# Agent attention with a gated convolution on one core: fold order, agent-value tiles and the agents' table changed

## The chip, the cores and the metric

The kernel runs on 1 core of one Trainium2 chip. The time is device microseconds of one execution; 431.86 us is the median of 3 runs before the change (431.13 to 434.68). The engines are TensorE (PE, with its weight loads listed apart as PEld), VectorE (DVE), ScalarE (ACT), GpSimd (POOL) and SyncE (SP), which issues most of the DMAs.

## The reference

Two stages. In the attention, 49 agents look at 12,800 keys and gather values; then 12,800 queries look at the 49 agents and take their gathered values. The result goes through a causal depthwise convolution of 5 taps, a sigmoid gate and two 128 x 128 matrices. Batch 4, 128 channels, all float32 in and out.

```python
def sm(a, b):
    s = scale * (a @ b.transpose(0, 2, 1))
    s = s - s.max(-1, keepdims=True)
    e = np.exp(s)
    return e / (e.sum(-1, keepdims=True) + 1e-09)
a2k = sm(agents, k)
agent_v = a2k @ v
q2a = sm(q, agents)
x = q2a @ agent_v
...
for k in range(K):
    gate_pre += conv_w[k][None, None, :] * xp[:, k:k + S, :]
gate = 1.0 / (1.0 + np.exp(-gate_pre))
val = x @ w_val
return (gate * val @ w_out).astype(np.float32)
```

## The kernel before

The sequence of each batch is cut into 10 units of 1280 positions (`UNIT`) and 25 chunks of 512 (`CH`). The attention output x is never formed in 128 channels. It is q2a @ agent_v, so agent_v (49 rows) is folded into the weights that follow: the fold builds, per batch, matrices of 49 agents by 128 channels for each convolution tap and for the value matrix, and the chunks multiply the 49 normalised query weights by them. Each is split into two float16 parts, stacked in the rows of one matmul.

For the program a unit or chunk of work has a letter, and the list `work` holds them in the order of PE:

- `("k", b, u)`, `key_scores`: 8 matmuls with 32-column weights (half the 64 padded agents, four groups of 320 keys in four column tiles of the PE array side by side) into one of two PSUM banks `sc`, which alternate from one score unit to the next. ACT copies the bank to `ks`, DVE takes the maximum (`kmx`).
- `("v", b, u)`, `agent_values`: ACT's exponentials `e`, DVE's 32 x 32 block transposes `eT`, then 10 matmuls of 128 rows by 64 columns (one per block of 128 keys) by 129 value columns, the last of them ones for the denominator. They accumulate in `av`; even blocks go to PSUM rows 0 to 63, odd ones to 64 to 127.
- `("q", b, u)`, `queries`: scores as for the keys, then on DVE sT (transposes, which free the `sc` bank), qmx, on POOL the subtraction, on ACT the exponential, on DVE qsm, qr and the product qw, and the two float16 parts pt by ACT and POOL.
- `("t", b, u)`, `transposes`: pt into x1. The first four units (`PE_FIRST`) by 10 PE transposes into an `sc` bank, which ACT and DVE copy out; the others by a DMA transpose. Five DMAs (`shifts`) then copy 20 rows of x1, each shifted by a tap, to x2.
- `("fold", b)`, one of five steps of `fold_weights`: (1) `av` is copied (L491), halves are added by two matmuls, DVE normalises to `avT`, POOL makes `gw`, DVE the gate's scale. (2) PE multiplies by the value matrix, and DVE and ACT write the split weights `wst`. (3) PE transposes `wst` 8 times, DVE and ACT copy to `stat`; POOL scales the output matrix to `wo`. (4) PE transposes `wo` (L629); DVE finds its scale and splits it into `wsp` (L634 to L643). (5) PE transposes `wsp` twice (L655), DVE copies to `wo16`.
- `("g", t)`, `("a", t)`, `("o", t - 2)`: gate and value matmuls of a chunk (they need `stat`; the value matmuls write the bank `val`, read by DVE's `h`, L868), and the projection two chunks later, which needs `wo16`. The small PSUM results of batch 0's fold use the banks `out`, `val` and `gate` in turn.

`Plan` sets the order of the other engines: it simulates a list schedule with the given durations, with PE kept in the order of `work` and each change of a step's `key` on PE charged 0.12 us, and issues the steps by their start in that plan. The loads (k, q, v units) follow the order of `work` through 11 slots (`NLOAD`), issued from SP up to 11 units ahead; 8 DMAs may be out at a time in the plan.

For batch 0, all 10 key units run first, then two query units, then 10 value units. The fold of batch 0 is followed directly by chunk 0. `KEYS_FIRST` says how many of batch 1's key units stand ahead of the others around that fold. The keys of the next batch are spread over the early chunks of this one, its values over the later ones, two value units behind a score unit at five places (`at[AV0 + u // 2]`).

Of the kernel before, what the change touches and what calls it, by code (L numbers as in the profile page):

```python
# [19 lines left out]
BLK = 32  # L20
# [21 lines left out]
EARLY = ((1, 4), (2, 5), (4, 6))  # L42
SINGLE = 4
KEYS_EARLY = 2
KEYS_FIRST = 2
AV0 = 4
PE_FIRST = 4
PE_TURNS = ()
# [123 lines left out]
def tile_agent_attention_gated_conv(  # L172
# [81 lines left out]
    fold = const.tile([P, AP_], F32, name="fold")  # L254
    ag_sb = const.tile([P, B, AP_], F32, name="ag_sb")
    tiny = const.tile([P, NBLK], F32, name="tiny")
    nc.sync.dma_start(out=ag_sb, in_=agT.rearrange("b c a -> c b a"))
    make_identity(nc, ident)
    make_identity(nc, ident16)
    nc.vector.tensor_tensor(  # L260
# [88 lines left out]
    def load(kind, b, u):  # L349
        i = taken[0] % NLOAD  # L350
        taken[0] += 1
        slot_of[kind, b, u] = i
        if kind == "v":
            dst, src = ld[i], vP[b, u].rearrange("p n c -> p (n c)")
        else:
            dst = ld[i][:, 0:UNIT]
            src = (kT if kind == "k" else qT)[b, :, u * UNIT : (u + 1) * UNIT]
        add("dma", 0.4, lambda: nc.sync.dma_start(out=dst, in_=src), (), [("ld", i)], 1.57)

    def score_matmuls(b, src, out):  # L360
        for j in range(2):
# [10 lines left out]
    def transpose_blocks(out, in_):  # L372
        nc.vector.transpose(  # L373
            out=out.rearrange("p n (j i) -> p j n i", j=2),
            in_=in_.rearrange("p j (n i) -> p j n i", i=BLK),
        )


    def key_scores(b, u):
        i = slot_of["k", b, u]  # L380
        ps, at = bank()
        km = ("kmx", b % 2)
        add("pe", 1.07, lambda: score_matmuls(b, ld[i], ps), [("ld", i)], [at], key="sc")

        first = b == 0 and u == NU - 1

        def copy():
            add(
                "act", 0.64, lambda: nc.scalar.copy(out=ks[:, u], in_=ps[:, :, 0:GT]),  # L389
                [at] + ([(*km, u)] if first else []), [("ks", u)],  # L390
            )

        if not first:
            copy()
        src = ps[:, :, 0:GT] if first else ks[:, u]
# [52 lines left out]
    def agent_values(b, u):  # L448
# [8 lines left out]
                    bias=kbias[b % 2][:, j : j + 1], scale=SCALE,  # L457
                )

        def matmuls():  # L460
            for n in range(NBLK):
                o = (n % 2) * AP_
                nc.tensor.matmul(  # L463
                    out=av[o : o + AP_, 0 : C + 1], lhsT=et[:, n, :], rhs=vt[:, n, :],
                    start=(u == 0 and n < 2), stop=(u == NU - 1 and n >= NBLK - 2),
                )

        add("act", 1.0, exps, [("ks", u), ("kbias", b % 2)], [("e", u % 2)])
        add("dve", 0.84, lambda: transpose_blocks(et, e), [("e", u % 2)], [("eT", u % 3)])
        add(  # L470
            "pe", 1.07, matmuls, [("eT", u % 3), ("ld", i)], ["av"], key="av"
        )


    av2 = const.tile([P, C + 1], F32, name="av2")
# [191 lines left out]
    def queries(b, u):  # L667
# [7 lines left out]
        add("pe", 1.07, lambda: score_matmuls(b, ld[i], ps), [("ld", i)], [at], key="sc")  # L675
# [270 lines left out]
    for u in range(NU):  # L946
        work.append(("v", 0, u))
        if u == T_AT:
            work.append(("t", 0, 0))
    work += [("fold", 0), ("k", 1, 0), ("fold", 0), ("k", 1, 1), ("fold", 0)]  # L950
    after = {
        0: [("fold", 0), ("q", 0, 2), ("fold", 0), ("t", 0, 1), ("q", 0, 3)],
        1: [("t", 0, 2)],
        2: [("t", 0, 3)],
    }
# [6 lines left out]
    for b in range(B):  # L962
# [6 lines left out]
        if b + 1 < B:  # L969
            u0 = KEYS_FIRST if b == 0 else KEYS_EARLY  # L970
            part = (NU - u0 + 3) // 4
            for n, u in enumerate(range(u0, NU)):
                before[t0 + at[n // part]].append(("k", b + 1, u))
            for t in MAX_AT:
                behind[t0 + t].append(("max", b + 1))
            for u in range(NU):
# [81 lines left out]
```

## Time and profile before

| what | us |
|---|---|
| median of 3 runs | 431.86 |
| runs | 431.13 to 434.68 |
| profiled execution, whole | 431.22 |
| its span, first to last instruction | 429.4 |
| PE busy in the span | 402.9 |
| DVE / ACT / POOL busy | 297.0 / 300.4 / 224.3 |

The span is what the profile's times count from; the profiled execution's own time is 1.8 us longer. A row of the timeline or of the chain gives the start, the length, engine, what is written and read with its line, and a count where equal instructions were merged; in brackets stands the idle time before it and what ended it. Matmuls overlap, so lengths of merged rows run past the start of the next row. A float32 matmul is recorded twice, with two weight loads.

### The profile page before, as it was taken

How to read it: one execution, taken by the hardware profiler on the slowest of the kernel's cores; microseconds unless marked ns; L12 is line 12 of the kernel's file. 1: busy time of each engine (PE TensorE's matmuls, PEld its weight loads, DVE VectorE, ACT ScalarE, POOL GpSimd, SP SyncE). 2: the span in 40 equal slices, each digit the busy share in tenths (PEclk: the TensorE clock that was granted, in tenths of full speed). 3: DMA queues.
4: the chain of work that ended last, by engine and by line, in shares of the span. 5: the costliest groups of instructions: out<-in, count | busy, mean ns of one | idle time of the engine just before them, and what ended most of it. 6: DMA issues, size and time to landing. Idle time of an engine off the chain costs nothing.

```text
span 429.4 us, 8968 instructions
## 1 busy us (share of the span) xinstructions
PE 402.9 (94%) x3307; PEld 194.8 (45%) x3307; DVE 297.0 (69%) x555; ACT 300.4 (70%) x520; POOL 224.3 (52%) x239
## 2 busy tenths in 40 slices
PE   3978888999999999999999999999999999999995
PEld 1357333345565444444555544445555544434443
DVE  3776879886786877578666887678666787566231
ACT  1464536678976577778876676778876577777875
POOL 1002246564466665544557665553356466687553
PEclk9999989999999999999999999999999999999999
DMA  8999999999999999999999999999999999887743
GB/s 288 422 415 415 371 350 337 297 285 309 343 358 294 249 270 289 307 309 305 340 329 356 292 323 292 320 312 334 306 330 257 289 291 287 215 199 173 192 156 122
DMA packets 76158, 128.07 MB, mean 298 GB/s; under 512 B 51644, under 2 KB 51900, under 8 KB 76116
## 3 DMA queue, kind: packets, MB, share of 16 engines
q1 hardware_dynamic: 76056, 127.41, 96.0%
q8 instruction: 26, 0.43, 0.4%
q14 instruction: 16, 0.13, 0.1%
q10 hardware_dynamic: 60, 0.10, 0.1%
HBM read 79.25 MB, written 26.21 MB: 246 GB/s over the span
## 4 chain that ended last, share of the span: by engine, by line
PE 65%; DMA 13%; DVE 12%; ACT 5%; issue 3%; SPq 1%; POOL 1%; DVEq 0%; ACTq 0%; POOLq 0%
PE gate L828 20%; PE sc L363 13%; PE av L463 6%; PE gate L832 4%; PE val L855 4%; PE val L859 4%; PE out L898 4%; PE out L899 4%; PE out L900 4%; DMA ld<-qT 3%; DMA ld<-vP 3%; DVE h L868 2%; ACT e L455 2%; DMA ld<-kT 2%; DMA outT<-ob 2%
## 5 line engine op out<-in xcount | busy, mean ns | idle before, releaser
L879 POOL TENSOR_TENSOR hl<-h,hh 128x512 f16<-128x512 f32 (+1 forms) x101 | 117.0, 1160 | 121.3 <-ACT hh L874 113.7
L828 PE MATMUL gate<-x,stat 128*128 128x512 f16 (+1 forms) x500 | 124.4, 378 | 2.4 <-ACT th L841 2.3
L868 DVE SCALAR_TENSOR_TENSOR h<-th,val 128x512 f32<-128x512 f32 x100 | 67.7, 677 | 69.1 <-PE out L899 46.1
L363 PE MATMUL sc<-ld,ag_sb 128*32 128x320 f32 x1280 | 102.0, 452 | 10.0 <-DMA ld<-kT 8.0
L912 ACT ACTIVATE ob<-out,oscale 128x512 f32<-128x512 f32 x98 | 67.2, 686 | 23.5 <-PE out L900 17.4
L841 ACT ACTIVATE th<-gate,unscale 128x512 f32<-128x512 f32 x100 | 68.3, 683 | 19.7 <-PE gate L832 18.0
L828 PEld LDWEIGHTS <-stat 128*128 128x128 f16 x505 | 45.6, 97 | 66.4 <-issue 19.0
L874 ACT CAST hh<-h 128x512 f16<-128x512 f32 (+1 forms) x101 | 61.4, 608 | 13.1 <-DVE h L868 12.4
L684 POOL TENSOR_TENSOR qw<-sT,qmx 128x490 f32<-128x490 f32 x40 | 41.5, 1038 | 50.2 <-DVE qmx L679 50.1
L363 PEld LDWEIGHTS sc<-ld,ag_sb 128*32 128x32 f32 x1280 | 37.0, 112 | 62.8 <-issue 22.5
L463 PE MATMUL av<-ld,eT 128*64 128x129 f32 x800 | 49.5, 275 | 1.7 <-DMA ld<-vP 1.4
L389 ACT COPY ks<-sc 128x640 f32<-128x640 f32 x40 | 27.7, 691 | 32.7 <-PE sc L363 30.6
L463 PEld LDWEIGHTS av<-ld,eT 128*64 128x64 f32 x800 | 43.7, 136 | 11.7 <-issue 7.3
L726 POOL TENSOR_TENSOR pt<-qw,pt 128x490 f16<-128x490 f32 x40 | 44.7, 1119 | 3.8 <-ACT pt L713 3.1
L455 ACT ACTIVATE e<-ks,kbias 128x320 f32<-128x320 f32 x80 | 39.0, 553 | 6.1 <-DVE kbias L444 3.3
L373 DVE STREAM_TRANSPOSE eT<-e 128x640 f32<-128x640 f32 x40 | 33.6, 842 | 11.4 <-ACT e L455 5.9
L373 DVE STREAM_TRANSPOSE sT<-sc 128x640 f32<-128x640 f32 x40 | 33.3, 834 | 10.8 <-PE sc L363 10.6
L398 DVE TENSOR_REDUCE kmx<-ks 128x2 f32<-128x640 f32 x39 | 31.4, 817 | 11.8 <-ACT ks L389 11.8
L832 PE MATMUL gate<-x,stat 100*128 100x512 f16 x100 | 38.0, 380 | 0.8 <-DMA x<-x 0.8
L855 PE MATMUL val<-x,stat 128*128 128x512 f16 x100 | 37.8, 378 | 0.1
L859 PE MATMUL val<-x,stat 100*128 100x512 f16 x100 | 37.8, 378 | 0.0
L898 PE MATMUL out<-hh,wo 128*128 128x512 f16 x98 | 37.1, 379 | 0.0
(125 smaller groups left out, 392.1 us busy)
## 6 DMA issues: line engine op xcount, KB each, us to landing
ld<-vP SPq DMA_DIRECT2D x40, 645.0 KB
ld<-kT SPq DMA_DIRECT2D x40, 640.0 KB
ld<-qT SPq DMA_DIRECT2D x40, 640.0 KB
outT<-ob SPq DMA_DIRECT2D x48, 512.0 KB
x<-x SPq DMA_DIRECT2D x90, 100.0 KB
x<-x SPq DMA_DIRECT2D x18, 50.0 KB
outT<-ob SPq DMA_DIRECT2D x3, 256.0 KB
x<-pt SPq DMA_TRANSPOSE x36
```

Of the source, the lines that this page charges most:

```text
L363: nc.tensor.matmul(out=out[g * BLK : (g + 1) * BLK, j, 0:GT], lhsT=ag_sb[:, b, j * BLK : (j + 1) * BLK], rhs=src[:, g * GT : (g + 1) * GT] ...
L373: nc.vector.transpose(out=out.rearrange("p n (j i) -> p j n i", j=2), in_=in_.rearrange("p j (n i) -> p j n i", i=BLK),)
L463: nc.tensor.matmul(out=av[o : o + AP_, 0 : C + 1], lhsT=et[:, n, :], rhs=vt[:, n, :], start=(u == 0 and n < 2), stop=(u == NU - 1 and n >= ...
L828: nc.tensor.matmul(out=pg, lhsT=stat[:, k, :], rhs=x1[:, c : c + w], start=(k == 0), stop=False,)
L832: nc.tensor.matmul(out=pg, lhsT=stat[0 : TAPS * X2R, TAPS + 1, :], rhs=x2[0 : TAPS * X2R, o2 : o2 + w], start=False, stop=True,)
L841: lambda: nc.scalar.activation(out=th, in_=pg, func=AF.Tanh, scale=unscale[:, 0:1]),
L855: nc.tensor.matmul(out=pv, lhsT=stat[:, TAPS, :], rhs=x1[:, PAD + n0 : PAD + n0 + w], start=True, stop=False,)
L859: nc.tensor.matmul(out=pv, lhsT=stat[0 : TAPS * X2R, TAPS + 2, :], rhs=x2[0 : TAPS * X2R, o2 : o2 + w], start=False, stop=True,)
L868: lambda: nc.vector.scalar_tensor_tensor(out=h, in0=th, scalar=1.0, in1=pv, op0=ALU.add, op1=ALU.mult),
L874: "act", 0.16 + 0.42 * scale, lambda: nc.scalar.copy(out=hh, in_=h),
L879: lambda: nc.gpsimd.tensor_tensor(out=hl, in0=h, in1=hh, op=ALU.subtract),
L912: lambda: nc.scalar.activation(out=ob[:, o : o + w], in_=po, func=AF.Copy, scale=oscale),
```

## The change

Six things:

1. The agents' table is stored as c x b x a, and its load is issued by ACT, not SP.
2. The load of the last value unit of batch 0 is split into two halves (a second key `ld2`), and its 10 blocks into two steps on PE, each waiting for its half.
3. The agent-value matmuls use two 32-column tiles in place of one of 64, so 20 in place of 10 per unit, with tile positions like the scores'. Their `key` in the plan becomes that of the scores, "sc".
4. Around batch 0's fold: `("q", 0, 2)` moves from behind chunk 0 to behind the second fold step; the key unit `("k", 1, 2)` stands behind the third in place of ahead of chunk 0, and `("k", 1, 3)` behind chunk 0.
5. The fourth fold step (the transpose of `wo`) moves ahead of chunk 0's gate.
6. The other key units of batch 1 start one place later (`at[n // part + (b == 0)]`).

```diff
-KEYS_FIRST = 2
+KEYS_FIRST = 4
...
-    nc.sync.dma_start(out=ag_sb, in_=agT.rearrange("b c a -> c b a"))
+    nc.scalar.dma_start(out=ag_sb, in_=agT)
...
-        add("dma", 0.4, lambda: nc.sync.dma_start(out=dst, in_=src), (), [("ld", i)], 1.57)
+        parts = [(dst, src, [("ld", i), ("ld2", i)])]
+        if (kind, b, u) == ("v", 0, NU - 1):
+            h = VW // 2
+            parts = [(dst[:, 0:h], src[:, 0:h], [("ld", i)]), (dst[:, h:], src[:, h:], [("ld2", i)])]
+        for d, f, keys in parts:
+            add(
+                "dma", 0.4, lambda d=d, f=f: nc.sync.dma_start(out=d, in_=f), (), keys,
+                1.57 / len(parts),
+            )
...
-        def matmuls():
-            for n in range(NBLK):
+        def matmuls(blocks):
+            for n in blocks:
                 o = (n % 2) * AP_
-                nc.tensor.matmul(
-                    out=av[o : o + AP_, 0 : C + 1], lhsT=et[:, n, :], rhs=vt[:, n, :],
-                    start=(u == 0 and n < 2), stop=(u == NU - 1 and n >= NBLK - 2),
-                )
+
+                for j in range(0, AP_, BLK):
+                    nc.tensor.matmul(
+                        out=av[o + j : o + j + BLK, 0 : C + 1],
+                        lhsT=et[:, n, j : j + BLK], rhs=vt[:, n, :],
+                        start=(u == 0 and n < 2), stop=(u == NU - 1 and n >= NBLK - 2),
+                        tile_position=(0, o + j),
+                    )
...
-        add(
-            "pe", 1.07, matmuls, [("eT", u % 3), ("ld", i)], ["av"], key="av"
-        )
+        h = HB if (b, u) == (0, NU - 1) else NBLK
+        first = range(0, h)
+        add(
+            "pe", 1.07 * h / NBLK, lambda: matmuls(first),
+            [("eT", u % 3), ("ld", i)] + [("ld2", i)] * (h == NBLK), ["av"], key="sc",
+        )
+        if h < NBLK:
+            add(
+                "pe", 1.07 * (1 - h / NBLK), lambda: matmuls(range(h, NBLK)),
+                [("eT", u % 3), ("ld2", i)], ["av"], key="sc",
+            )
...
-    work += [("fold", 0), ("k", 1, 0), ("fold", 0), ("k", 1, 1), ("fold", 0)]
+
+    work += [("fold", 0), ("k", 1, 0), ("fold", 0), ("q", 0, 2), ("k", 1, 1), ("fold", 0), ("k", 1, 2), ("fold", 0)]
     after = {
-        0: [("fold", 0), ("q", 0, 2), ("fold", 0), ("t", 0, 1), ("q", 0, 3)],
+        0: [("fold", 0), ("t", 0, 1), ("q", 0, 3), ("k", 1, 3)],
...
-                before[t0 + at[n // part]].append(("k", b + 1, u))
+                before[t0 + at[n // part + (b == 0)]].append(("k", b + 1, u))
...
-    agT = np.zeros((b, c, AP_), agents.dtype)
-    agT[:, :, :a] = agents.transpose(0, 2, 1)
+    agT = np.zeros((c, b, AP_), agents.dtype)
+    agT[:, :, :a] = agents.transpose(2, 0, 1)
```

PE, from the first fold step of batch 0 to the first of the stat transposes (`out` and `val` are the fold's small banks, `sc0` and `sc1` the score banks, `ld0` to `ld2` the slots of the units). Before:

```order
L494 MATMUL out_132<-fold_138,av2_157 128x64
L498 MATMUL out_132<-fold_138,av2_157 128x64
L363 MATMUL sc0_128<-ld0_61,ag_sb_139 32x320 x8
L536 MATMUL val_131<-avT_159,moe_sb_155 128x49
L363 MATMUL sc1_129<-ld1_62,ag_sb_139 32x320 x8
L593 LDWEIGHTS wst0_118
L593 MATMUL gate_130<-ident16_137,wst0_118 128x128
```

In this order the two score units are the keys 0 and 1 of batch 1. The same place now:

```order
L514 MATMUL out_132<-fold_138,av2_157 128x64
L518 MATMUL out_132<-fold_138,av2_157 128x64
L371 MATMUL sc0_128<-ld0_61,ag_sb_139 32x320 x8
L556 MATMUL val_131<-avT_159,moe_sb_155 128x49
L371 MATMUL sc1_129<-ld1_62,ag_sb_139 32x320 x8
L371 MATMUL sc0_128<-ld2_63,ag_sb_139 32x320 x8
L613 LDWEIGHTS wst0_118
L613 MATMUL gate_130<-ident16_137,wst0_118 128x128
```

Three score units stand there; the second, from `ld1`, is query unit 2. Next on PE, before, from the last value matmul of chunk 0 to the transposes of `wsp`:

```order
L859 LDWEIGHTS stat0_120
L859 MATMUL val_131<-x20_100,stat0_120 128x512
L629 MATMUL out_132<-ident_136,wo_163 128x128
L363 MATMUL sc0_128<-ld4_65,ag_sb_139 32x320 x8
L655 LDWEIGHTS wsp_165
L655 MATMUL val_131<-ident16_137,wsp_165 128x128
```

Before, the transpose of `wo` and query unit 2 stood between chunk 0 and `wsp`. Now, from the last stat transpose to the first gate matmul:

```order
L613 LDWEIGHTS wst0_118
L613 MATMUL gate_130<-ident16_137,wst0_118 128x128
L371 MATMUL sc1_129<-ld3_64,ag_sb_139 32x320 x8
L649 MATMUL out_132<-ident_136,wo_163 128x128
L848 LDWEIGHTS stat0_120
L848 MATMUL gate_130<-x1_99,stat0_120 128x512
```

One key unit and the transpose of `wo` stand ahead of the gate, and the transposes of `wsp` follow chunk 0 directly. DVE, behind the last write of `wst` (qsm1 and qw1 belong to query unit 1, `kmx1` to the keys of batch 1). Before:

```order
L613 TENSOR_SCALAR unscale0_124<-mx_160 128x2
L697 TENSOR_REDUCE qsm1_93<-qw1_90 128x10
L698 SCALAR_TENSOR_TENSOR qsm1_93<-qsm1_93,tiny_140 128x10
L701 RECIPROCAL qr1_95<-qsm1_93 128x10
L604 COPY stat0_120<-gate_130 128x512
L706 TENSOR_TENSOR qw1_90<-qw1_90,qr1_95 128x490
L398 TENSOR_REDUCE kmx1_74<-ks_72 128x2 x4
L868 SCALAR_TENSOR_TENSOR h0_106<-th0_103,val_131 128x512
L373 STREAM_TRANSPOSE sT0_85<-sc0_128 128x2x10x32
L634 TENSOR_REDUCE oscale0_126<-out_132 128x1
```

There the four key maxima stood ahead of `h0` and of the scale of `wo`. Now:

```order
L381 STREAM_TRANSPOSE sT0_85<-sc1_129 128x2x10x32
L633 TENSOR_SCALAR unscale0_124<-mx_160 128x2
L717 TENSOR_REDUCE qsm1_93<-qw1_90 128x10
L718 SCALAR_TENSOR_TENSOR qsm1_93<-qsm1_93,tiny_140 128x10
L721 RECIPROCAL qr1_95<-qsm1_93 128x10
L624 COPY stat0_120<-gate_130 128x512
L726 TENSOR_TENSOR qw1_90<-qw1_90,qr1_95 128x490
L654 TENSOR_REDUCE oscale0_126<-out_132 128x1
```

The block transpose of query unit 2 comes first, and the scale of `wo` directly behind qw1; the key maxima follow later. Beyond the first eight chunks the order on PE, DVE, ACT and POOL is as before, apart from the tiles; on SP, rows change places with their neighbours through three batches.

More of the change, by code (lines that the diff above doesn't have):

```diff
@@ L382, in key_scores @@
         km = ("kmx", b % 2)
-        add("pe", 1.07, lambda: score_matmuls(b, ld[i], ps), [("ld", i)], [at], key="sc")
+        add("pe", 1.07, lambda: score_matmuls(b, ld[i], ps), [("ld", i), ("ld2", i)], [at], key="sc")
         first = b == 0 and u == NU - 1
@@ L674, in queries @@
         sa = sT[:, :, 0:A]
-        add("pe", 1.07, lambda: score_matmuls(b, ld[i], ps), [("ld", i)], [at], key="sc")
+        add("pe", 1.07, lambda: score_matmuls(b, ld[i], ps), [("ld", i), ("ld2", i)], [at], key="sc")
         add("dve", 0.84, lambda: transpose_blocks(sT, ps[:, :, 0:GT]), [at], [("sT", x)])
```

## The prediction

> **What bounds the kernel.** I read the page first, then the busy time by stretch, then the chain of work that ended last, and at the end the timeline of TensorE (PE) in short windows. From the page, the span, the busy time of each engine and the granted clock in 40 slices:
>
> ```profile
> span 429.4 us, 8968 instructions
> PE 402.9 (94%) x3307; PEld 194.8 (45%) x3307; DVE 297.0 (69%) x555; ACT 300.4 (70%) x520; POOL 224.3 (52%) x239
> PEclk9999989999999999999999999999999999999999
> ```
>
> 94% is a mean over stages, so the stretches (microseconds from the start; per engine busy time and instructions, then clock and DMA share):
>
> ```profile
> 20.00:40.00 20.00, 16.18 (x238) 11.40 (x232) 15.40 (x25) 12.12 (x26) 2.56 (x3) 1.00 1.02 417
> 40.00:60.00 20.00, 16.39 (x187) 8.28 (x187) 14.98 (x42) 8.24 (x15) 5.68 (x7) 0.93 1.02 393
> 57.30:60.60 3.30, 3.30 (x25) 0.90 (x18) 2.90 (x6) 1.25 (x3) 0.55 (x2) 0.50 1.02 424
> 60.00:90.00 30.00, 27.66 (x243) 11.32 (x243) 26.53 (x44) 20.71 (x35) 18.61 (x21) 0.99 0.99 306
> 90.00:140.00 50.00, 50.00 (x431) 26.59 (x425) 36.20 (x59) 39.11 (x71) 29.36 (x31) 1.00 1.00 317
> 290.00:340.00 50.00, 49.45 (x423) 26.13 (x420) 35.51 (x57) 37.61 (x69) 26.72 (x28) 1.00 1.05 306
> ```
>
> From 90 us on PE is never idle: a matmul or a gap saved there shortens the end. Before 40 us the DMA queues bound (417 GB/s, share 1.02). Between 40 and 90 us PE loses 3.6 and 2.3 us idle, and 3.3 us at half clock. The 8 in the clock row is that last stretch. The chain, in order of time (start, length, what), shows the end of the DMA stage and the one behind it:
>
> ```profile
> 25.14 12.70 DMA ld<-vP
> 37.97 1.32 PE av L463 x20
> 39.29 0.67 PE sc L757 x10
> 39.96 2.52 PE av L463 x40
> ...
> 42.50 0.30 DVE av L491
> ...
> 47.43 0.61 PE gate L593 x8
> 48.04 2.29 PE sc L363 x32
> 50.33 1.19 PE gate L828 x5
> ...
> 52.28 1.26 PE sc L363 x16
> ...
> 56.60 3.80 PE sc L363 x32
> 60.39 1.32 PE gate L828 x5
> ```
>
> **The change, part by part.** The sum is made against the profiled execution, 431.22 us (span 429.4 and 1.8 around it); the median of the three runs is 0.64 above that, so a measured gain will read about 0.6 larger against that median.
>
> *Agents' table and last values.* SyncE (SP) issues at the start:
>
> ```profile
> 0.74 0.47 SPq L257 DMA_DIRECT2D ag_sb<-agT  x1
> 1.26 0.49 SPq L326 DMA_DIRECT2D ob<-moe  x1
> 1.80 5.51 SPq L358 DMA_DIRECT2D ld<-kT  x9
> ```
>
> With the table on ScalarE's queue, the first key unit is issued at 1.26 instead of 1.80, 0.54 us sooner, and the DMA stage that follows runs at its rate until 37.84. Lower end 0 (the wires, not the issue, set the start), upper end 0.54 and a little for fewer packets; I take 0.45, because the row that bounds this stage is an issue queue feeding a full wire. ScalarE's own issue (0.47 by SP's row) costs nothing: its first copy waits for the first scores anyway. Splitting the last value unit adds one issue of about 0.4 and one wait; the 40 agent-value matmuls took 2.52 here, 0.17 more than the 2.35 of the same group later (row below), so at most 0.17 is to be had. I take 0.1. Together -0.55.
>
> *Fold and first chunks.* Times here are microseconds after the copy of `av` at 42.50. Before: stat transposes at +4.9, two key units, first gate at +7.8, scores of q2 at +9.8 to +11.0, a wait, t1, two score units to +17.9, second gate. These rows of PE, then VectorE (DVE), price it:
>
> ```profile
> 47.43 0.61 PE L593 MATMUL gate<-ident,wst 128*128 128x128 f16 x8 [1.14 <-DVE wst L548]
> 55.42 0.23 PE L655 MATMUL val<-ident,wsp 128*128 128x128 f16 x1 [1.92 <-DVE wsp L642]
> 69.90 0.73 PE L757 MATMUL sc<-ident,pt 128*128 128x128 f16 x10 [1.21 <-POOL pt L726]
> 52.52 0.68 DVE L868 SCALAR_TENSOR_TENSOR h<-th,val 128x512 f32<-128x512 f32 x1
> 53.57 0.85 DVE L373 STREAM_TRANSPOSE sT<-sc 128x640 f32<-128x640 f32 x1 [0.37 <-PE sc L363]
> 54.34 0.25 DVE L634 TENSOR_REDUCE oscale<-out 128x1 f32<-128x128 f32 x1
> 55.40 0.35 DVE L643 SCALAR_TENSOR_TENSOR wsp<-out,ro,wsp 128x128 f16<-128x128 f32 x1
> 55.67 0.65 DVE L679 TENSOR_REDUCE qmx<-sT 128x10 f32<-128x490 f32 x1
> ```
>
> Now q2's scores fill the 1.14 us wait before the stat transposes, which stay at +4.9 because DVE's `wst` releases them. k2 then needs the bank of q2, which DVE empties behind `wst`: +4.85 and 0.85 gives +5.7, so k2 ends at +6.9 and the transpose of `wo` stands ahead of the gate. DVE's copy of `stat` is queued behind that sT, so the gate starts at about +7.4, where it was +7.8. Next DVE does qw (0.7, estimated from h, the same size), the scale of `wo` and `wsp` (54.34 to 55.75, 1.4), qmx 0.65 and h 0.68: +10.8. The transposes of `wsp` write the bank that h reads, so they come at +10.8 instead of +12.9: the old wait of 1.92 shrinks to some 1.6, it isn't gone. Behind them wait t1, then three score units (q3, k3, q4) where there were two. Three in a row cost 3.47 (row below) and end at +15.1 if nothing holds them; but k3 needs the bank of t1, emptied by ScalarE and DVE behind h (till about +13.2, estimated as four more operations of h's length), and q4 the bank that DVE's sT of q3 empties (sums of some 1.1 and sT 0.85 later, +15.1). So the second gate comes at +16.3, where it was +17.9: -1.6. What is late next is again DVE. Its queue now holds the query chain ahead of two of the four key maxima, so pt of the fourth unit should be ready and the 1.21 wait at 69.90 go, while q5's sT costs a new 0.75: another -0.45. I take -2.0. Lower end 0 (DVE, 26.53 busy of 30 us, gives the time back), upper end -3.5 (scores unheld, and the waits of 1.14, 1.92 and 1.21 gone). The moved loads are issued in the new order of use, four of them ahead of the same shift DMAs on SP as before. q2 is now loaded before k1 and k2, which each land one load later (645 KB at 417 GB/s, 1.55 us) and are used one score unit later (1.2 us), so 0.35 us of slack goes there. I cost it at nothing: the eighth value unit lands at 37.84 (25.14 + 12.70), two more and k0 and k1 behind it at 1.55 each make 44.0 for k1, and it is read at about +2.5, 45.0; were that slack gone, the fold would lose 0.35.
>
> *Agent values in 32-column tiles.* Short windows of PE, and its weight loads, at one group of scores followed by agent values:
>
> ```profile
> 98.66 0.72 PE L363 MATMUL sc<-ld,ag_sb 128*32 128x320 f32 x8
> 98.93 0.45 PE L363 MATMUL sc<-ld,ag_sb 128*32 128x320 f32 x4
> 99.31 0.33 PE L463 MATMUL av<-ld,eT 128*64 128x129 f32 x2
> 101.45 0.28 PE L463 MATMUL av<-ld,eT 128*64 128x129 f32 x2
> 101.67 0.39 PE L828 MATMUL gate<-x,stat 128*128 128x512 f16 x1
> 98.39 0.13 PEld L363 LDWEIGHTS sc<-ld,ag_sb 128*32 128x32 f32 x4
> ```
>
> And two pieces of the chain, two units of agent values and three units of scores:
>
> ```profile
> 99.38 2.35 PE av L463 x40
> ...
> 158.00 3.47 PE sc L363 x48
> ```
>
> Groups of four score matmuls start 0.27 apart (98.66, 98.93); the first agent-value pair starts 0.38 after the last group and lasts 0.33 where a later one lasts 0.28. So going from 32 to 64 columns costs 0.11 + 0.05 = 0.16, by rounded figures; I take 0.15. Leaving for the gate costs 0.1 (101.45 to 101.67 against a pair's 0.11) and stays, whatever the tile. With one width the entry should cost nothing, as between the three score units that take 3.47 together, 1.16 each. It stands at 5 places in each of 3 batches: 15 x 0.15 = 2.2. In batch 0 it hides behind DMA. The work itself stays: a unit's 20 records of 64 columns, two at a time, become 40 of 32 columns, four at a time, so ten steps of 129 rows either way, about 1.17 us a unit, if four run side by side as the scores' do. Lower end 0 (gap stays), upper end 2.4. I take -2.2, since the nearest row, scores behind scores, shows no such gap.
>
> On that doubling the Trainium skill (TensorE: Matmul & The Clock Gate, section "Wait — 56ns, not 53.3ns?") speaks against the change: starts of matmuls never come closer than about 25 ns. By that figure 40 matmuls need an estimated 1.0 us a unit, which just fits; if the weight loads took turns on it as well, 2.0 us. The trace differs for weight loads of separate column tiles: four of them, start to end, lie within 0.13 us in the row at 98.39.
>
> Sum: 431.22 - 0.55 - 2.0 - 2.2 = 426.5 us.
>
> **Rivals.** (a) Issue-bound narrow tiles, the one on the slower side. PE is fed 80 instructions a unit instead of 40. The densest stretch shown is 80 records in 2.35 us, 29 ns each; whether PE takes them faster for two units on end no row shows. If 29 ns were its pace, a unit would take 2.35 instead of 1.17 us: +47, about 475. It decides from 4.75 / 1600 = 3 ns on each added instruction. Against it: the scores' loads come four in 0.13 us, though in bursts. The skill's floor named above is this rival in another form. (b) The clock falls again. The half-clock row at 57.3 follows the wait at 55.42 and then transposes; now +9.2 to +11.6 holds a wait and transposes alone. Half clock on the next three scores adds about 1.5: 428.0. The Trainium skill (same page, section "Part 4: PE-mode transpose") says transposes do not count as activity; the trace agrees in that the clock fell after such a stretch. (c) DVE gives the fold's gain back by 90 us: 428.5. (d) The gap at 98.93 isn't one of tile width and stays: 428.7.
>
> **How the numbers follow.** Forecast as summed 0.52, (a) 0.10, (b) 0.13, (c) 0.13, (d) 0.12. Three terms each with ends of 0 to their upper bound make the likeliest case 424.5 to 428. The range reaches over (b), (c) and (d) with two small misses together, 423.8 to 430.2, and leaves out (a) and the worst that the reordered SP queue may do. A measurement of this kernel can tell about 1% from no change, and 1% under the median of 431.86 is 427.5. The forecast lies below that four times in five (0.42), and of (b) to (d) a quarter do (0.10): faster 0.52; slower is (a), 0.10; the same takes the rest, 0.38.
>
> **What would show it.** Right: the first 40 agent-value records of a group behind scores start 0.27 after the last four scores; a pair of units takes 2.35 or less; the first key scores start near 6.6 us instead of 7.1; the wait for `wsp` is about 1.6; the second gate starts near 58.2, and PE is full again some 2.5 us sooner. Wrong: a group of four agent values over 0.12 us; PE's row of the clock with a second 8; DVE over 28 us busy between 57 and 87 with PE waiting for sT; SP holding a load behind a shift or an output.

## The result: slower by one per cent

The changed kernel takes 437.26 us (median of 22 runs, 433.61 to 441.65), the kernel before 432.44 in the same runs (429.76 to 435.64). The ratio is 1.0101, 95% interval 1.0078 to 1.0124: some 4.4 us slower, where 426.5 was forecast. The profiled execution shown below took 435.36. Medians and ranges here count every run, ratios leave disturbed executions out; the profile of the first experiment (439.79, far over that kernel's median) is one, so of it only the value stage of batch 0 is read.

From the page of the changed kernel: span, busy time by engine, the granted clock by slice, the instruction queue, and the groups of agent values and of output copies (busy, mean ns, idle time before them and what ended it).

```profile
span 433.3 us, 10570 instructions
PE 400.6 (92%) x4107; PEld 196.2 (45%) x4107; DVE 296.4 (68%) x555; ACT 299.9 (69%) x520; POOL 225.9 (52%) x239
PEclk9989999999999999999999999999999999999999
q8 instruction: 32, 0.52, 0.5%
L473 PE MATMUL av<-ld,eT 128*32 128x129 f32 x1600 | 48.0, 273 | 4.7 <-issue 4.7
L932 ACT ACTIVATE ob<-out,oscale 128x512 f32<-128x512 f32 x98 | 67.1, 685 | 32.0 <-DMA outT<-ob 17.6
```

PE is busy 2.3 us less than before in a span 3.9 us longer. Two new waits stand here: 4.7 us in which the agent values waited for "issue", and 17.6 us of ACT for output buffers (4.1 before). There are 1,602 more instructions and 6 more fetches on the instruction queue than in the page of before:

```profile
q8 instruction: 26, 0.43, 0.4%
```

That is 267 instructions for a fetch of some 16 KB. PE's timeline of the changed kernel at the end of batch 0's value stage:

```profile
33.37 3.73 PE L473 MATMUL av<-ld,eT 128*32 128x129 f32 x127 [0.21 <-issue]
39.63 1.52 PE L473 MATMUL av<-ld,eT 128*32 128x129 f32 x44 [2.53 <-issue]
41.07 0.73 PE L777 MATMUL sc<-ident,pt 128*128 128x128 f16 x10
41.74 2.19 PE L473 MATMUL av<-ld,eT 128*32 128x129 f32 x72
45.86 0.43 PE L473 MATMUL av<-ld,eT 128*32 128x129 f32 x8 [1.94 <-issue]
```

Between the two stalls lie 44 + 10 + 72 = 126 matmuls, each with a weight load: 252 instructions, about one fetch. In the window from 37.1 to 39.7 us, the first stall, the view of the DMA queues (packets, MB, share of 16 engines) shows the loads' queue full and one fetch, 0.027 x 16 x 2.6 = 1.1 us of packet time:

```profile
q1 hardware_dynamic: 319, 1.05, 102.2%
q8 instruction: 1, 0.02, 2.7%
```

The first key scores start at 5.86 (7.10 before), yet the copy of `av` comes at 46.35 (42.50 before). The stretches of the changed kernel, columns as in the prediction, and below them the stretch from 240 us of the kernel before:

```profile
40.00:60.00 20.00, 15.92 (x263) 9.09 (x252) 14.09 (x41) 7.45 (x13) 5.71 (x7) 1.00 0.94 363
60.00:90.00 30.00, 28.68 (x264) 11.98 (x261) 28.28 (x49) 21.76 (x37) 20.33 (x21) 1.00 0.92 288
90.00:140.00 50.00, 50.00 (x631) 27.43 (x630) 36.15 (x60) 39.31 (x71) 30.04 (x32) 1.00 1.01 303
240.00:290.00 50.00, 46.64 (x372) 20.16 (x370) 35.85 (x72) 33.41 (x57) 27.21 (x29) 1.00 1.05 310
```

```profile
240.00:290.00 50.00, 49.21 (x397) 21.46 (x396) 37.35 (x76) 36.59 (x61) 29.16 (x31) 1.00 1.04 315
```

The DMA share between 40 and 90 us falls from 1.02 and 0.99 to 0.94 and 0.92. Later the queues are full, as before, and PE, idle 0.79 us between 240 and 290 us before, is now idle 3.36 there.

### The profile page after: what moved, and what is told of

Same layout as the page of the kernel before. It is cut to its first block, busy times and chain, and to the rows that moved or that the text cites. A ratio compares the mean times of both kernels' runs of the same rounds, so it can differ in the third digit from the quotient of the medians.

```text
span 433.3 us, 10570 instructions
## 1 busy us (share of the span) xinstructions
PE 400.6 (92%) x4107; PEld 196.2 (45%) x4107; DVE 296.4 (68%) x555; ACT 299.9 (69%) x520; POOL 225.9 (52%) x239
## 4 chain that ended last, share of the span: by engine, by line
PE 61%; DMA 13%; DVE 12%; ACT 8%; issue 4%; POOL 1%; SPq 0%; ACTq 0%; DVEq 0%
PE gate L848 19%; PE sc L371 12%; PE av L473 8%; DMA outT<-ob 6%; DMA ld<-kT 5%; PE val L875 4%; PE gate L852 4%; PE val L879 4%; PE out L918 3%; PE out L919 3%; PE out L920 3%; ACT e L463 3%; DVE h L888 3%; DMA x<-pt 2%; ACT th L861 2%
## 5 line engine op out<-in xcount | busy, mean ns | idle before, releaser
L932 ACT ACTIVATE ob<-out,oscale 128x512 f32<-128x512 f32 x98 | 67.1, 685 | 32.0 <-DMA outT<-ob 17.6
L704 POOL TENSOR_TENSOR qw<-sT,qmx 128x490 f32<-128x490 f32 x40 | 42.4, 1060 | 47.5 <-DVE qmx L699 47.2
L473 PE MATMUL av<-ld,eT 128*32 128x129 f32 x1600 | 48.0, 273 | 4.7 <-issue 4.7
L473 PEld LDWEIGHTS av<-ld,eT 128*32 128x32 f32 x1600 | 44.7, 109 | 10.0 <-issue 5.6
L746 POOL TENSOR_TENSOR pt<-qw,pt 128x490 f16<-128x490 f32 x40 | 45.6, 1142 | 2.9 <-ACT pt L733 2.3
L406 DVE TENSOR_REDUCE kmx<-ks 128x2 f32<-128x640 f32 x39 | 31.4, 814 | 12.1 <-ACT ks L397 12.0
```

The lines of the kernel that those rows point to most:

```text
L473: nc.tensor.matmul(out=av[o + j : o + j + BLK, 0 : C + 1], lhsT=et[:, n, j : j + BLK], rhs=vt[:, n, :], start=(u == 0 and n < 2), stop=(u ...
L932: lambda: nc.scalar.activation(out=ob[:, o : o + w], in_=po, func=AF.Copy, scale=oscale),
```

## The experiments

### First four: which part costs

The theory from the two profiles, F: PE ran out of instructions, because 32-column tiles double the records while the loads fill the queues. The rivals: a cost of the tiles themselves, or of the fold's order.

```diff
 e1, e2: the changed kernel
+                step = AP_                            # e1
+                step = AP_ if b == 0 else BLK         # e2
+                for j in range(0, AP_, step):
 e3: the kernel before, with the changed kernel's loop over BLK columns only
 e4: the kernel before, with the changed lists of `work`, `after`, `before` and KEYS_FIRST = 4 only
```

Without narrow tiles anywhere:

> The changed kernel, with the agent values in one 64-column tile again; the plan, and so the order of every engine, stays that of the changed kernel. Fetch theory (32-column tiles double PE's instructions in the value stage of batch 0, and PE runs dry of them there while the DMA wires are full: stalls of 2.5 and 1.9 us that nothing releases): both stalls go, the copy of av comes near 42 us instead of 46.3, the later groups lose the 0.15 us of entry again, and the time is 1 to 2.5 us under the changed kernel, about 434.5 to 436 by medians. Rival (the split load of the last values, or the table on ScalarE's queue, holds the stage): the stalls stay, the copy of av stays near 46, and the time is about 2 us over the changed kernel. Order theory (SP's new order makes outputs late): ScalarE still waits some 15 us in all for outputs.

Narrow tiles from batch 1 on:

> The changed kernel, with 64 columns in batch 0 and 32 in batches 1 to 3; orders as in the changed kernel. Fetch theory: the copy of av comes near 42 us, the later groups keep 2.20 us, and the time is 3.5 to 4.5 us under the changed kernel, about 433. Rival (narrow tiles are as good in batch 0, the stage is held by a load): within 1 us of the changed kernel. Order theory: ScalarE still waits some 15 us for outputs, and the kernel is no faster than the one before by more than 1 us.

Narrow tiles alone:

> The kernel before, with 32-column tiles for the agent values and nothing else; the order of every engine is that of the kernel before. Fetch theory: PE stalls twice by some 2 us in the value stage, the copy of av comes 3 to 4.5 us later than 42.5, the entries give 2.2 back, and the time is 1 to 2.5 us over the kernel before. Rival (the stalls come of the split load or the table's queue): no such stall, 2.2 us under the kernel before. Order theory: ScalarE's wait for outputs stays near the 4 us of before.

The fold's order alone:

> The kernel before, with the new order of the fold alone (items 4 to 6 of the change); agent values in 64 columns, table and loads as before. SP's order then differs from before in most of the places in which the changed kernel's does. Order theory: the fold gives 2 to 4.5 us by 90 us of the span, and waits for outputs take 3 to 5 back behind 190 us: within 1.5 us of the kernel before, ScalarE's wait for outputs 12 us or more. Rival (the late waits come of something else, such as the tiles): the gain of 2 to 4.5 us stays to the end.

| run | median us | ratio to before, 95% |
|---|---|---|
| e1_no_tiles | 432.31 | 1.0001 (0.9966 to 1.0036) |
| e2_tiles_late | 435.70 | 1.0086 (1.0047 to 1.0124) |
| e3_tiles_alone | 438.84 | 1.0153 (1.0091 to 1.0215) |
| e4_fold_alone | 433.31 | 1.0036 (1.0003 to 1.0069) |

The stalls come with the narrow tiles of batch 0 and with nothing else. PE's timeline of e3:

```profile
34.24 3.73 PE L464 MATMUL av<-ld,eT 128*32 128x129 f32 x127 [0.34 <-issue]
40.53 1.51 PE L464 MATMUL av<-ld,eT 128*32 128x129 f32 x44 [2.57 <-issue]
46.77 0.43 PE L464 MATMUL av<-ld,eT 128*32 128x129 f32 x8 [1.94 <-issue]
```

And of e1, where units of the same stage wait at most 0.3 us and `av` is copied at 41.43:

```profile
35.46 1.32 PE L471 MATMUL av<-ld,eT 128*64 128x129 f32 x20 [0.26 <-DMA ld<-vP]
37.05 1.32 PE L471 MATMUL av<-ld,eT 128*64 128x129 f32 x20 [0.27 <-DMA ld<-vP]
```

So F holds, but it is not all: e2 has no such stalls and is still slower (F forecast about 433), and the fold's order, which had its first gates ahead of before, is no gain. In e4 ACT waits 12.1 us for output buffers. Two more of F's forecasts missed: e1 came out below 434.5 to 436 us, and e3 loses 6.6 us by its ratio, from 4 runs, where 1 to 2.5 were forecast.

### Second four: SP's order

The plan gives SP another order when the fold changes. Theory S: this order costs time, because outputs are issued later and ACT waits in order for their buffers. Rival D: the queues are full, so any lead of PE goes back to them. A table of SP's steps forces one kernel's SP order on another; e8 doubles the matmuls of batch 0 without narrow tiles.

```diff
+SP_ORDER = """..."""
+        lists["dma"].sort(key=lambda i: place[plan.tags[i]])
 e5: e4's kernel, SP in before's order from the load of q4 on
 e6: the kernel before, SP in e4's order from the same load on
 e7: e2's kernel, SP in before's order from the same load on
 e8: the kernel before
+                for c0, c1 in ((0, 65), (65, C + 1)) if b == 0 else ((0, C + 1),):
+                        out=av[o : o + AP_, c0:c1], lhsT=et[:, n, :], rhs=vt[:, n, c0:c1],
```

> The new fold order alone, as in the run before it of that name, but behind the first shift DMAs SP's rows stand in the order of the kernel before; PE, VectorE, ScalarE and GpSimd keep the order of the fold run. Order theory (the place of outputs among SP's waiting DMA transposes makes them late, and ScalarE stops at the output buffer): ScalarE's wait for outputs falls from 12.1 to about 5 us, the lead of 4 us over the kernel before that stands at the eighth chunk stays to the end, and the time is 2.5 to 4.5 us under the kernel before. Rival (the wires are full whatever SP's order, so that a lead is given back to the DMA queues): the lead melts as before, ScalarE waits 10 us or more, and the time is within 1.5 us of the kernel before.

> The kernel before, with nothing changed but SP's rows behind the first shift DMAs, which take the order of the fold run; every other engine keeps the order before. Order theory: chunks 0 to 30 as before, then waits for outputs of 10 us or more and 3 to 8 us slower than before. Rival (full wires, no matter the order): within 1 us of the kernel before, waits for outputs near 4 us.

> The changed kernel with 64 columns in batch 0 and 32 later, and SP's rows behind the first shift DMAs in the order of the kernel before. Order and fetch theories: both losses are gone, 4 us of lead at the eighth chunk and 2.2 from the entries stay: 425.5 to 427.5, 5 to 6 us under the kernel before. Rival (full wires): no better than 430.5.

> The kernel before, with 64-column tiles, but in batch 0 each agent-value matmul cut into two of 65 and 64 value columns: as many PE instructions there as with 32-column tiles, the same columns streamed, no tile of 32 columns in that stage. Fetch theory: PE stalls with no releaser about every 256 instructions (2 to 2.7 us, twice) as with narrow tiles, and the copy of av comes 3 to 5 us later than 42.5. Rival (the narrow tile itself stalls, by its weight loads or four streams): no such stalls, the copy of av within 1.5 us of 42.5.

| run | median us | ratio to before, 95% |
|---|---|---|
| e5_fold_sp_before | 432.10 | 0.9992 (0.9953 to 1.0030) |
| e6_sp_order_alone | 435.42 | 1.0068 (1.0029 to 1.0107) |
| e7_best | 432.56 | 0.9970 (0.9926 to 1.0014) |
| e8_halved_values | 435.71 | 1.0082 (1.0039 to 1.0125) |

e8 settles that the count of instructions makes the stalls, and not the narrow tile: 64-column tiles, twice the instructions, stalls at the same counts. That PE waits there for the next block of instructions is inferred, from the counts and from the fetch beside the stall; no run changed the fetch itself.

```profile
40.09 1.61 PE L464 MATMUL av<-ld,eT 128*64 128x65 f32 x44 [2.24 <-issue]
46.11 0.46 PE L464 MATMUL av<-ld,eT 128*64 128x65 f32 x8 [1.45 <-issue]
```

e6 shows that SP's order alone costs 0.7%. How, SP's own rows tell. The kernel before, then e6:

```profile
49.06 1.15 SPq L358 DMA_DIRECT2D ld<-kT  x2
50.30 1.37 SPq L358 DMA_DIRECT2D ld<-qT  x2
51.76 0.38 SPq L358 DMA_DIRECT2D ld<-kT  x1
57.88 3.79 SPq L791 DMA_DIRECT2D x<-x  x5
```

```profile
49.22 0.86 SPq L392 DMA_DIRECT2D ld<-kT  x2
50.17 0.38 SPq L392 DMA_DIRECT2D ld<-qT  x1
59.14 3.79 SPq L825 DMA_DIRECT2D x<-x  x5
63.03 0.42 SPq L392 DMA_DIRECT2D ld<-qT  x1
63.55 0.84 SPq L392 DMA_DIRECT2D ld<-kT  x2
```

Before, five loads go out from 49.06 on, ahead of the shifts that wait for DVE's copy of x1. In e6 three do, and SP stands from 50.6 to 59.1 with loads that could go behind it. The queues run half empty; one stretch of before, then of e6:

```profile
56.00:62.00 6.00, 6.00 (x51) 2.33 (x49) 4.77 (x10) 1.94 (x4) 2.55 (x3) 0.72 0.97 388
```

```profile
56.00:62.00 6.00, 5.16 (x46) 2.14 (x47) 4.70 (x13) 1.92 (x3) 1.89 (x4) 0.72 0.52 201
```

The two orders differ at later places too, through three batches, so that the loss comes from this one place is argued, not shown. And e5, with before's order, only equals before (S forecast 2.5 to 4.5 us less, and 5 to 6 less for e7): S doesn't explain why the fold's lead is worth nothing that the runs can tell. The times of e5 and e7 are as rival D has them; e6, 2.9 us slower, lies nearer to S (3 to 8) than to D (within 1).

### Third four: output buffers, and the late tiles alone

```diff
 e9: the kernel before
+                step = AP_ if b == 0 else BLK
 e10: e5's kernel; e11: the kernel before, its orders kept; e12: e6's kernel
-NOB = 3
+NOB = 4
```

> The kernel before with one edit: 32-column matmuls for the agent values of the second to the fourth batch only; the first batch, the fold, the agents' table and every order are those of before. If narrow tiles cost only through the instructions that the first batch's unit work runs out of, this must be faster: some 15 entries less 0.15 us each, a ratio near 0.995, and no row of av waiting for issue. If doubling the matmuls has a price of its own in the later batches (more records to be fetched through queues that are full), it is slower, as the version with late tiles was beside the one with none: 435.7 against 432.3, a ratio near 1.008. At 1.000 the gain of the entries is given back inside the batches.

> The fold's new order with SP's order of before, as in the earlier run, and four output buffers where there were three; no engine's order changes. ScalarE waited 6.6 us for output buffers in that run (5 times, the longest 2.9). If these waits are where the fold's lead goes, the ratio falls from 0.999 to 0.985 to 0.992 (432.1 less 3 to 6.6 us). If the lead goes to the transfers in general, it stays near 0.999 and the wait turns up at another tile.

> The kernel before with four output buffers and its own orders on all engines. ScalarE waited 4.1 us in 2 places for them before. If every wait of ScalarE for an output buffer is paid in full, about 428 (ratio 0.990); if it is hidden or taken up by the next wait, 1.000. It is the ground against which the runs with four buffers are read.

> The kernel before with the new SP order from the ninth key load on, which alone gave a ratio of 1.0068 with 13.5 us of waits of ScalarE for output buffers, and now four output buffers. If the new SP order costs time because outputs leave later and ScalarE waits in order for their buffers, a fourth buffer brings it back to that of before with four buffers, within 0.2%. If the order costs elsewhere (later key or query loads, the transposes), it stays 0.5% or more above it.

| run | median us | ratio to before, 95% |
|---|---|---|
| e9_late_tiles_alone | 432.92 | 1.0010 (0.9974 to 1.0046) |
| e10_fold_four_outputs | 431.85 | 0.9981 (0.9953 to 1.0009) |
| e11_before_four_outputs | 432.83 | 0.9983 (0.9945 to 1.0020) |
| e12_sp_order_four_outputs | 435.10 | 1.0058 (1.0021 to 1.0094) |

The second half of S, the wait for buffers, falls. With four buffers ACT waits at most 0.3 us for an output to leave, and the SP order costs as much (e12 against e11). The wait only moves. From the waits of e5, then of e10 (total, times, longest):

```profile
ACT pt L747 <- DMA x<-pt: 3.5, 1, 3.5
ACT pt L747 <- DMA x<-pt: 9.6, 3, 4.6
```

Bytes moved sort the profiles: GB/s of the stretches times their lengths, up to 140 us, give for before 349 x 20 + 417 x 20 + 393 x 20 + 306 x 30 + 317 x 50 = 48.2 MB. Every kernel with before's SP order and no stall (e5, e7, e9, e10, e11) has 48.0 to 48.4 MB and a ratio of 0.997 to 1.001; e6 has 45.7, e12 46.3, the changed kernel 46.7, e4 46.9, e2 47.2, e3 47.4 and e8 47.5, with ratios from 1.004 to 1.015. Inside that second group the bytes don't rank them, and e1, whose profile doesn't count here, has the new SP order and a ratio of 1.0001.

### Fourth four: fewer bytes

If the queues are a second bound beside PE, taking bytes away must bring the lost gains back. Each output store sends half of its columns, so half of the output stays unwritten; the page then shows 114.97 MB for 128.07. No engine's order changes.

```diff
-                out=outT[b, :, n0 + w - n : n0 + w], in_=ob[:, lo : lo + n]
+                out=outT[b, :, n0 + w - n : n0 + w - n + n // 2], in_=ob[:, lo : lo + n // 2]
```

On the kernel before (e13), on e5's (e14), e9's (e15) and e6's (e16):

> The kernel before with its own orders; each output store sends half of its columns, so half of the output is left unwritten and 12.8 of 128 MB are not moved. Nothing else changes. If the transfers carry the middle of the kernel together with TensorE, this is faster by what TensorE waits there: 4.5 us idle from 90 to 390 us, about 427.5, ratio 0.990. If TensorE alone bounds it, it stays at 1.000. It is the ground for the three beside it.

> The fold's new order with SP's order of before (its ratio was 0.999 with full outputs), storing half of each output. If the fold's lead of about 4 us is given back because transfers are as far as before, it is now kept: 3 to 5 us below the kernel before with half outputs. If it goes to something else (VectorE, the order inside the gates), it stays within 1 us of it.

> 32-column tiles in the second to the fourth batch (ratio 1.001 alone), storing half of each output. If the gain at the entries was real and was given back to the transfers, about 2 us below the kernel before with half outputs; if narrow tiles have a price of their own, at or above it.

> The kernel before with the new SP order (ratio 1.0068, and 1.0058 with four output buffers), storing half of each output. If the order costs because the transfers stand idle between 40 and 90 us (they had moved 45.7 MB by 140 us where before had moved 48.2) and full queues never make that up, there is now room to make it up, and it comes within 1 us of the kernel before with half outputs. If its cost lies in one late tile that engines wait for, it stays 2 to 3 us above.

And two for the sum, the changed kernel (e17) and e7's, the one without stalls and with before's SP order (e18):

> The changed kernel as it is, storing half of each output. If the account is complete, the parts add to the kernel before with half outputs (428.5): the fold less 3.1, narrow tiles of the later batches less 2.1, the new SP order 0, the agents' table 0, and the instructions that the first batch's narrow tiles run out of, 3.5 to 4 more: 426.8 to 427.5, so faster than the kernel before on the same footing. If the changed kernel has another cost, it is above 428.5.

> The changed kernel with 64-column tiles in the first batch and SP's order of before (its ratio was 0.997 with full outputs), storing half of each output. With the parts as measured one by one: 428.5 less 3.1 less 2.1, and the table between 0 and 1.2: 422.1 to 423.3. Its distance to the changed kernel with half outputs is the price of the instructions that the first batch runs out of: 3.5 to 4 us.

| run, half outputs | median us (range) | ratio to before with full outputs, 95% | less e13, us |
|---|---|---|---|
| e13_half_out_before | 428.53 (428.25 to 429.10) | 0.9903 (0.9872 to 0.9934) | |
| e14_half_out_fold | 425.47 (424.27 to 426.25) | 0.9832 (0.9795 to 0.9868) | -3.06 |
| e15_half_out_late_tiles | 426.39 (425.99 to 427.08) | 0.9854 (0.9819 to 0.9889) | -2.14 |
| e16_half_out_sp_order | 428.66 (428.04 to 429.71) | 0.9906 (0.9877 to 0.9935) | +0.13 |
| e17_half_out_after | 426.14 (425.02 to 427.32) | 0.9857 (0.9828 to 0.9886) | -2.39 |
| e18_half_out_mended | 422.22 (421.52 to 423.27) | 0.9770 (0.9740 to 0.9800) | -6.31 |

All six come out as D says; e17 lies 0.7 us below the window that was forecast. The last column is the difference of medians. e17 and e18 ran later than the other four, on another chip, where the kernel before took 432.10 us and not 432.77; by the ratios they lie 2.0 and 5.7 us below e13. A stretch of e13, then one of the kernel before and the same of e13:

```profile
240.00:290.00 50.00, 49.21 (x397) 21.45 (x396) 37.40 (x77) 36.31 (x61) 28.56 (x30) 1.00 1.04 292
340.00:390.00 50.00, 48.08 (x291) 20.67 (x290) 35.77 (x75) 35.80 (x62) 33.71 (x35) 1.00 0.97 243
340.00:390.00 50.00, 48.87 (x296) 21.15 (x295) 35.73 (x76) 36.89 (x64) 34.65 (x35) 1.00 0.64 141
```

PE's idle time between 340 and 390 us falls from 1.92 (before) to 1.13, and the queues have room at the end. From 240 to 290 us the share is 1.04 as before, so the share alone doesn't tell whether there is room. Added up from 90 to 390 us, PE is idle 4.5 us in the kernel before, 5.7 in e5, 7.2 in e9 and 11.0 in e7, and 3.4 to 3.8 in all six with half outputs; e11 has 7.2 without any lead, so one execution's sum is rough. Some 0.8 us of what e13 gains on the kernel before is the shorter end behind the last matmul (3.2 us against 4.0). The fold's lead is now kept. DVE's copies of `av` in batches 0 and 1, of e13, e14, e17 and e18:

```profile
42.60 0.29 DVE L491 COPY av<-av 128x129 f32<-128x129 f32 x1 [1.27 <-PE av L463]
140.00 0.29 DVE L491 COPY av<-av 128x129 f32<-128x129 f32 x1 [0.78 <-PE av L463]
```

```profile
42.49 0.29 DVE L525 COPY av<-av 128x129 f32<-128x129 f32 x1 [1.27 <-PE av L497]
137.17 0.29 DVE L525 COPY av<-av 128x129 f32<-128x129 f32 x1 [0.78 <-PE av L497]
```

```profile
44.92 0.29 DVE L511 COPY av<-av 128x129 f32<-128x129 f32 x1 [3.29 <-PE av L473]
137.51 0.29 DVE L511 COPY av<-av 128x129 f32<-128x129 f32 x1 [0.65 <-PE av L473]
```

```profile
41.88 0.29 DVE L545 COPY av<-av 128x129 f32<-128x129 f32 x1 [1.15 <-PE av L507]
134.47 0.29 DVE L545 COPY av<-av 128x129 f32<-128x129 f32 x1 [0.65 <-PE av L507]
```

e13 to e14: 140.00 to 137.17, -2.83, and last matmuls at 423.30 and 420.49. e17 and e18 part by 3.04 us in batch 0 and stay parted by it: the price of the stalls, which are 1.48 and 1.94 us in e17's profile. By medians it is 3.92; e17 has the new SP order too, which costs 0.13 in e16. One term is left over: 428.53 - 3.06 - 2.14 = 423.33 and e18 is at 422.22, so 1.1 us (0.6 by the ratios, some 2 by the last matmuls of the profiles) goes to the table, the split load and the planner's key of the agent values, which were not taken apart.

## Why the prediction was wrong

**The step that failed first: "From 90 us on PE is never idle: a matmul or a gap saved there shortens the end."** The same rows showed a DMA share of 0.99 to 1.05, and one of them PE at 49.45 us of 50, which is not "never idle"; I took the queues for the bound before 40 us only. The transfers bound the middle beside PE. With all bytes, the fold's order on before's SP order gave 0.9992 and the late tiles 1.0010; with a tenth less, -3.06 and -2.14 us. Both gains were real on PE, and with all bytes the intervals of the two runs allow at most 2.0 and 1.1 us of them. This is why the gains are not paid; that the change loses comes of the next two steps that failed, batch 0's stalls and SP's queue.

**Narrow tiles: "In batch 0 it hides behind DMA."** The entries hide; the instructions don't. With twice the records in the stage that waits for loads, PE stands still twice: 2.53 and 1.94 us in the profile, 3.0 (traces) to 3.9 us (medians) on the end with half outputs, and 3.5 with all of them (e8, 1.0082). This is the term of batch 0 in the part on 32-column tiles, which I priced at 0.

**Narrow tiles, batches 1 to 3: right on PE.** -2.2 forecast; -2.14 with half outputs by medians, and by the traces of e13 and e15 -0.6 to -0.7 a batch. The chain's row in the changed kernel, where before had 2.35 for the pair of units:

```profile
98.72 2.21 PE av L473 x80
```

That is 0.14 an entry against 0.15, so rival (d) is out, and a unit's 40 matmuls stay at 1.1 us, so the pace of rival (a) is out too: 80 matmul records and their 80 weight loads, 160 instructions, in 2.21 us are 14 ns each, where that rival put 29. Rival (a) had the right sign, but its mechanism was a price on every added instruction; the cost is two stalls in one stage. On the rule that the prediction weighed, the Trainium skill (TensorE: Matmul & The Clock Gate, section "Wait — 56ns, not 53.3ns?"): with weight loads taking turns on its floor of about 25 ns between starts, a unit would have needed an estimated 2.0 us. The row shows 1.1, so loads don't take turns on it here.

**SP's queue: "I cost it at nothing."** The prediction followed the queue for q2, k1 and k2 only, and left "the worst that the reordered SP queue may do" out of the range. With full outputs it costs 0.68% (e6), 2.9 us; the rows of e6 show one place, a queue share of 0.52 between 56 and 62 us, and the prediction's own sign of error, "SP holding a load behind a shift". With half outputs it costs 0.13 us, though e16 is as far behind in bytes at 140 us (45.2 MB against 47.6 in e13).

**The fold: the steps came as worked out, their sizes did not, and that the sum is near is partly luck.** -2.0 forecast, -2.83 (trace) to -3.06 (medians). In the changed kernel the first gate comes 7.2 us after the copy of `av` (53.55 - 46.35; forecast 7.4) and the second 15.5 after it (61.83; forecast 16.3). The wait for `wsp` is 1.16 where 1.6 was forecast:

```profile
56.61 0.27 PE L675 MATMUL val<-ident,wsp 128*128 128x128 f16 x2 [1.16 <-DVE h L888]
60.61 1.28 PE L371 MATMUL sc<-ld,ag_sb 128*32 128x320 f32 x16 [0.45 <-DVE sT L381]
```

q4 waits 0.45 us for the bank of q3, as worked out. But the +17.9 of before, from which the -1.6 at the second gate was taken, holds the half-clock piece: its two score units took 3.80 us in the chain. e13, with before's orders and the full clock there, shows them and the second gate, and e14 its second gate:

```profile
56.61 2.66 PE L363 MATMUL sc<-ld,ag_sb 128*32 128x320 f32 x32
59.21 1.25 PE L828 MATMUL gate<-x,stat 128*128 128x512 f16 x5
```

```profile
58.59 1.25 PE L863 MATMUL gate<-x,stat 128*128 128x512 f16 x5
```

From the copies of `av` (42.60, 42.49) that is +16.6 and +16.1: against the same clock the fold's order is worth 0.5 at the second gate, 1.1 in the changed kernel, and not 1.6. What was too small is the rest, -0.45 after it: at the fourth gate e14 is 2.3 us ahead in all (68.42 against 70.79), at the end 2.8, and e13's waits for `pt`, 0.76 and 1.21 us, are gone. Rival (c), DVE giving it back, is out: the lead stays to the end where queues have room. Rival (b), the clock, didn't happen there; the 8 in the changed kernel's clock row is a half-clock piece from 25 to 28 us, which before has at 57. It was priced too high as well: counted from the copies of `av`, the kernel before, with that piece, is only 0.4 us behind e13 at the fourth gate, for e13 waits 0.76 for `pt` instead. The profiles of e14, e17 and e18 have, like e13's, no such piece between 40 and 60 us, so their differences to it hold no clock there; e15's and e16's have one (0.91 and 0.92).

**The table: -0.45 forecast.** The first scores come 1.24 us sooner, but the value stage behind them ends by its loads. With table and split load and no stalls `av` is copied at 41.43 (e1), 41.49 (e7), 41.88 (e18) and 43.17 (e2); without them at 42.36 to 42.88 in eleven profiles and 43.77 in one. So some 0.6 to 1 us is likely at that copy, for -0.55 forecast with the split; how much of it reaches the end, out of the 0.6 to 2 us left over above, stays open.

**The account.** With full outputs the changed kernel has two costs, stalls of 3.0 to 3.9 us and SP's order at 2.9 us, and loses 4.4: if the parts add up, of gains worth 5 us on PE some 1.5 to 2.4 are paid. With half outputs it beats the kernel before on the same footing by 2.0 (ratios) to 2.39 us (medians). Two things are not explained: e3, which loses 1.53% where e8, with as many instructions in batch 0, loses 0.82% and the late tiles alone next to nothing (e9; the intervals overlap), and e2, slower than e1 by 0.8% with full outputs, though e15 shows that late narrow tiles cost nothing themselves; e2 has them together with the new SP order on full queues, and no run takes that apart. No version that writes all of its output was faster than before by more than the runs can tell; the best, e7, is at 0.9970 (0.9926 to 1.0014).

## What to carry to other kernels

Read the DMA share in the same row as PE's busy share: where both are full, a saving on one may pay only if the other can move too, and taking a tenth of the bytes away in a trial tells which it is. Before taking a difference from one profile, look for a half-clock piece in it. Price a doubling of instructions not only by PE's pace but by where they are fetched: here PE stood still for them in the stage that loads at the full rate. When a list in the program changes, a planner changes the orders of queues far from it; look for loads that now stand behind a step that waits.

## What the runs showed of the hardware

- Instructions come over the same DMA engines as data, 0.52 MB in 32 fetches here, one for some 250 to 270 instructions. Beside loads at 102% share PE stood still 2.53 us beside a fetch with 1.1 us of packet time; where the other 1.4 us goes the records don't show. The second stall, 1.94 us from 43.92 on, came with the queues partly empty (share 0.76 from 44 to 50 us), so full queues are not its only condition. The Trainium skill (Runtime: NRT & Kernel Launch, section "Instruction fetch mechanics") says that a sequencer fetches blocks of 16 KiB, 256 instructions, while it executes the one before, at a cost "mostly hidden". The count agrees with the 252 between the stalls; if the stalls are such fetches, the cost was not hidden here: with 127 matmuls and their loads run through in 3.73 us, PE went on 2.53 us later.
- Halving 64 x 129 matmuls into 64 x 65 ones brought stalls at the same counts (2.24 and 1.45 us in e8) as halving the tiles (2.53 and 1.94): the count of instructions decides, not their form.
- Runs scatter less with half outputs: counting the executions that the ratios use, the six kernels with half outputs lie within 0.9 to 2.3 us each (4 to 6 runs), the twelve other experiments within 2.4 to 6.4 (4 to 12 runs). More runs make a wider range, so the sizes are rough.
